# Turning the attention output with VectorE and five transfers through DRAM instead of TensorE transposes

## The chip, the cores and the metric

The kernel runs on one core of a Trainium2 chip. The metric is device time in microseconds of one execution. Five engines work side by side, each on its own queue in order: TensorE (PE, with its weight loads PEld), VectorE (DVE), ScalarE (ACT), GpSimd (POOL) and SyncE (SP). Here SyncE issues nearly all transfers (DMAs), and 16 DMA engines carry them out.

## The reference

```python
B, S, D, Dff = 1, 2048, 576, 4608        # 32 heads of 18, window of 8 keys, dilation 2

xn = layernorm(x)
qkv = xn @ wqkv                          # 576 x 1728
idx = pos[:, None] - 2 * arange(8)       # keys at distance 0, 2, .. 14
attn = softmax(where(idx >= 0, q . k[idx] * 18 ** -0.5, -1e9))
o = sum_w attn * v[idx]
out = x + o @ wo + relu(xn @ w1) @ w2    # w1: 576 x 4608, w2: 4608 x 576
```

All inputs and outputs are float32.

## The kernel before

Rows of x are dealt to two phases (`NPH = 2`, even and odd positions, so that the dilation of 2 becomes a plain window inside a phase). A phase has 1024 rows as 8 tiles `i` of 128 rows, or 4 blocks `tb` of 256 rows. Every float32 factor of a product is split into a high part, rounded to the type float32r, and a low part, the rest; a product is three terms (high by high, low by high, high by low). As D = 576 = 4 x 128 + 64, a left operand of depth 576 is nine 128 x 128 pieces: `d[:, 0:4]` the high parts of the four full pieces, `d[:, 5:9]` their low parts, and `d[:, 4]` the last 64 columns with high parts in partitions 0 to 63 and low parts in 64 to 127. The list `TERMS` has the 14 pairs of pieces that are multiplied.

The time axis is a list of 288 steps (`slots`), 144 a phase: 12 chunks of 3 feed-forward column blocks `f`, over 4 row blocks `tb`. The program is written out by hand in this order. In step n, TensorE does `h_mm(n + 2)` (14 matmuls of 256 columns: a block of x times w1), then what `todo` has for the step, then `o_mm(n)` (12 matmuls of 288 columns: times w2, added up over the three f of a chunk), then what `todo_late` has. `h_mm`'s result is split by ScalarE (`hhi`, line 447) and VectorE (`hlo`, line 448). After f = 2, VectorE adds the chunk's sum to the tile x (line 471). The queues of all engines keep the order of emission.

Weights come through SyncE into `st` tiles (four buffers), three tasks ahead (`AHEAD = 3`), and are split by ScalarE (line 146) and VectorE (line 143) when their step comes: w1 five steps and w2 three steps before the chunk's step, and the five pieces of `wo` eight steps before the output projections. A load is issued when a task ahead of it has been split.

Attention runs on VectorE in four units a phase, as a background list `bg`, which `run_bg` feeds between the other work by an estimate of the time that each engine has been given (`t["pe"]`, `t["dve"]`) and a margin. The result o stands in `QO[ph]`, rows in partitions.

The output projection needs o with its columns in partitions. For each tile, `wo_a` makes a copy of the last 64 columns twice over (`od`, line 411, ScalarE) and calls `transpose_split` (line 264): five transposes of 128 x 128 by TensorE through PSUM (lines 273 and 274), from which ScalarE takes the high parts (lines 276 and 278) and VectorE the rest (lines 277 and 279) into `oT`. `wo_b` then does 28 matmuls of 288 columns, and VectorE adds the two halves to x (line 424). `done` sends a finished tile of x to DRAM.

In a phase that starts at step b, `wo_a(i)` is late in step b + 123 + i, and `wo_b(i)` one step later. In the last chunk of phase 0 (from step 132) the next phase's x is loaded (`load_x`, from step 129), its statistics and norms are taken (`stats`, `norm`, from steps 133 and 134) and it is transposed (`make_xt`, from step 136), on the same PSUM tiles `pm` (two buffers) as `wo_b`. The tile `xn` of `norm` has two buffers, x has 12.

Of the kernel before, what the change touches and what calls it, by code (L numbers as in the profile page):

```python
# [10 lines left out]
F32 = mybir.dt.float32  # L11
F32R = mybir.dt.float32r
AF = mybir.ActivationFunctionType
ALU = mybir.AluOpType
# [3 lines left out]
P = 128  # L18
# [9 lines left out]
EPS = 1e-5  # L28

UNIT0, UNIT_STEP, WO_AT = 7, 27, 8  # L30
HEADW = (-5, -2, -1, 0, 0, 1)

HEAD = (
# [22 lines left out]
def tile_body(ctx: ExitStack, tc: tile.TileContext, x, wqkv, wo, w1, w2, out):  # L56
    nc = tc.nc
    S, D = x.shape
# [5 lines left out]
    KT = 4  # L64
    DR = D - KT * P
    D2 = D // 2
# [4 lines left out]
    ctx.enter_context(tc.manual_schedule())  # L71
    pool = lambda name, bufs, **k: ctx.enter_context(tc.tile_pool(name=name, bufs=bufs, **k))
    consts = pool("consts", 1)
    xp = pool("xp", 12)
    xtp = pool("xtp", NTB)
    qop = pool("qop", 1)
    kp = pool("kp", 1)
# [7 lines left out]
    lgp = pool("lgp", 2)  # L85
    smp = pool("smp", 2)
    tmp = pool("tmp", 2)
    ps_o = pool("ps_o", 2, space=PSUM)
    ps_h = pool("ps_h", 2, space=PSUM)
    ps_m = pool("ps_m", 2, space=PSUM)  # L90

    f32 = lambda ap: ap.bitcast(F32)
# [18 lines left out]
    def mm(o, l, r, start, stop, n):  # L111
        nc.tensor.matmul(o, l, r, start=start, stop=stop)  # L112
        t["pe"] += n / 2400.0 + 0.002

    def dve(n):
        t["dve"] += (n + 130) / 960.0
# [134 lines left out]

    def norm(ph, i, act=False):
        nm, r = MR.pop((ph, i))
        xn = tmp.tile([P, 640], F32, name="xn")
        if act:
            nc.scalar.activation(xn[:, 0:D], X[ph, i], AF.Identity, bias=nm)  # L256
            nc.scalar.activation(xn[:, 0:D], xn[:, 0:D], AF.Copy, scale=r)  # L257
        else:
            nc.vector.tensor_scalar(xn[:, 0:D], X[ph, i], nm, r, op0=ALU.add, op1=ALU.mult)
            dve(600)  # L260
        nc.scalar.activation(xn[:, D:640], xn[:, KT * P : D], AF.Copy)
        XN[ph, i] = xn

    def transpose_split(src, last, hi, mix, lo, free=False):

        if free:
            pa, pb = (ps_o.tile([P, 2, 512], F32, name="po")[:, 0, :] for _ in range(2))
            pa, pb = pa.rearrange("p (k c) -> p k c", k=KT), pb[:, 0:P]
        else:
            pa = ps_m.tile([P, KT, P], F32, name="pm")  # L270
            pb = ps_m.tile([P, P], F32, name="pm")
        for k in range(KT):
            nc.tensor.transpose(pa[:, k, :], src[:, k * P : (k + 1) * P], ident)  # L273
        nc.tensor.transpose(pb, last, ident)  # L274
        t["pe"] += 5 * 0.06
        nc.scalar.activation(hi, pa, AF.Copy)  # L276
        nc.vector.tensor_tensor(lo, pa, f32(hi), op=ALU.subtract)
        nc.scalar.activation(mix, pb, AF.Copy)
        nc.vector.tensor_tensor(mix[DR:P], pb[DR:P], f32(mix[DR:P]), op=ALU.subtract)
        dve(512)  # L280
        dve(128)
# [10 lines left out]
    TERMS = [(k, k) for k in range(KT)] + [(5 + k, k) for k in range(KT)] + [(4, 4)] + [(k, 5 + k) for k in range(5)]  # L292
# [111 lines left out]

    OT = {}

    def wo_a(ph, i):
        assert (ph, i) in ready, (ph, i, len(bg))
        o = QO[ph][:, i, :]
        od = tmp.tile([P, 2, DR], F32, name="od")  # L410
        nc.scalar.activation(od, o[:, None, KT * P : D].to_broadcast([P, 2, DR]), AF.Copy)
        d = tmp.tile([P, 9, P], F32R, name="oT", bufs=1)
        transpose_split(o[:, 0:512], od.rearrange("p a b -> p (a b)"), d[:, 0:4, :], d[:, 4, :], d[:, 5:9, :])
        OT[ph, i] = d

    def wo_b(ph, i):
        d, w = OT.pop((ph, i)), WO[ph]
        po = [ps_m.tile([P, D2], F32, name="pm") for _ in range(2)]
        for j, (a, b) in enumerate(TERMS):
            for h in range(2):  # L420
                mm(po[h], d[:, a, :], w[b][:, h * D2 : (h + 1) * D2], j == 0, j == len(TERMS) - 1, D2)
        for h in range(2):
            acc = X[ph, i][:, h * D2 : (h + 1) * D2]
            nc.vector.tensor_tensor(acc, po[h], acc, op=ALU.add)
            dve(D2)
# [53 lines left out]
    def at(n, f, *a):  # L479
        todo.setdefault(n, []).append((f, a))  # L480
# [3 lines left out]
    def late(n, f, *a):  # L484
        todo_late.setdefault(n, []).append((f, a))

    plan = []
    for ph in range(NPH):
        b = ph * SPP
        for c in range(NCH):  # L490
            for f in range(C):
                s = b + c * SPC + f
                first = ph == c == 0
                plan.append((HEADW[f] if first else s - 5, w1_task, ((ph, c, f), c * C + f)))
                plan.append((HEADW[3 + f] if first else s - 3, w2_task, ((ph, c, f), c * C + f)))
        for u in range(NU):
            s = b + UNIT0 + u * UNIT_STEP
            plan.append((s - 5, wq_tasks, ((ph, u), u)))
            for i in range(NI):
                at(s + i, qkv_tile, ph, u, i)  # L500
            late(s + NI + 1, attention, ph, u)
        s = b + UNIT0 + NU * UNIT_STEP + WO_AT
        plan.append((s - 8, wo_tasks, (ph,)))
        for i in range(NI):
            late(s + i, wo_a, ph, i)
            at(s + i + 1, wo_b, ph, i)
            at(s + i + 1, done, ph, i)
        if ph + 1 < NPH:
            e = b + SPP - SPC
            for i in range(NI):  # L510
                z = e + 3 + 2 * i
                at(z - 6, load_x, ph + 1, i)
                late(z - 2, stats, ph + 1, i)
                late(z - 1, norm, ph + 1, i)
                at(z + 1, make_xt, ph + 1, i)
# [16 lines left out]
    held = []  # L532
    run_splits(-5)
    norm(0, 0)
    norm(0, 1)
    stats(0, 2)
    make_xt(0, 0)
# [48 lines left out]
```

## Time and profile before

| | |
|---|---|
| Time, median of 3 runs | 1194.78 us (1194.58 to 1195.4) |
| Profiled execution | 1194.74 us, span 1193.0 us |
| Mean granted TensorE clock | 0.998 |
| Busy: TensorE / VectorE / ScalarE / GpSimd | 99% / 68% / 26% / 3% |
| DMA, share of 16 engines | 19.7% SyncE's queue, 2.4% ScalarE's |

The span is the time between the first and the last record of the profiled execution; its time by the device's counter is 1.7 us longer. A busy share is an average over the whole span; what a stage waits for is read from that stage's own rows. The chain of waits goes back from the last instruction to what released each one, and so gives the work that set the end.

### The profile page before, as it was taken

How to read it: one execution, taken by the hardware profiler on the slowest of the kernel's cores; microseconds unless marked ns; L12 is line 12 of the kernel's file. 1: busy time of each engine (PE TensorE's matmuls, PEld its weight loads, DVE VectorE, ACT ScalarE, POOL GpSimd, SP SyncE). 2: the span in 40 equal slices, each digit the busy share in tenths (PEclk: the TensorE clock that was granted, in tenths of full speed). 3: DMA queues.
4: the chain of work that ended last, by engine and by line, in shares of the span. 5: the costliest groups of instructions: out<-in, count | busy, mean ns of one | idle time of the engine just before them, and what ended most of it. 6: DMA issues, size and time to landing. Idle time of an engine off the chain costs nothing.

```text
span 1193.0 us, 21739 instructions
## 1 busy us (share of the span) xinstructions
PE 1183.8 (99%) x9016; PEld 1172.8 (98%) x9016; DVE 812.5 (68%) x1269; ACT 310.5 (26%) x790; POOL 40.1 (3%) x63
## 2 busy tenths in 40 slices
PE   8999999999999999999999999999999999999998
PEld 7999999999999999999999999999999999999998
DVE  7516875888687578875573278858767875886732
ACT  5422222131222222322233123122221322222210
POOL 2000000010000000000120000000100000000000
PEclk9999999999999999999999999999999999999999
DMA  5312122130321311402242113031302312212002
GB/s 172 84 32 82 42 76 55 38 107 1 98 58 44 86 33 43 114 11 73 91 130 74 46 54 90 22 85 29 86 21 79 83 38 79 63 42 73 21 1 80
DMA packets 84883, 75.67 MB, mean 63 GB/s; under 512 B 6592, under 2 KB 68288, under 8 KB 84784
## 3 DMA queue, kind: packets, MB, share of 16 engines
q1 hardware_dynamic: 82256, 66.08, 19.7%
q10 hardware_dynamic: 2528, 8.20, 2.4%
q8 instruction: 71, 1.16, 0.4%
q14 instruction: 28, 0.23, 0.1%
HBM read 61.34 MB, written 4.72 MB: 55 GB/s over the span
## 4 chain that ended last, share of the span: by engine, by line
PE 98%; DVE 1%; SPq 0%; ACT 0%; DMA 0%; issue 0%; DVEq 0%; ACTq 0%
PE ph L112 39%; PE po L112 38%; PE pm L112 20%; PE pm L273 1%; PE pm L274 0%; DMA st<-in_w 0%; SPq L235 0%; DVE pr L380 0%; DVE pr L373 0%; SPq L157 0%; SPq L162 0%; SPq L161 0%; PE po L273 0%; ACT xn L257 0%; ACT xn L256 0%
## 5 line engine op out<-in xcount | busy, mean ns | idle before, releaser
L112 PE MATMUL ph<-xT,w1t 128*128 128x256 f32 x4032 | 514.2, 279 | 1.3 <-ACT xT L276 0.6
L112 PEld LDWEIGHTS ph<-xT,w1t 128*128 128x128 f32 x4032 | 491.6, 188 | 2.0 <-ACT xT L276 0.8
L112 PE MATMUL po<-w2t,hhi 128*128 128x288 f32 x2304 | 400.5, 296 | 0.4 <-DVE w2t L143 0.3
L112 PEld LDWEIGHTS po<-w2t,hhi 128*128 128x128 f32 x2304 | 337.0, 188 | 2.0 <-DVE w2t L143 0.5
L447 ACT ACTIVATE hhi<-ph 128x256 fp32r<-128x256 f32 x288 | 110.2, 382 | 531.8 <-PE ph L112 512.5
L112 PE MATMUL po<-w2t,hlo 128*128 128x288 f32 x1152 | 244.7, 293 | 0.0
L448 DVE SCALAR_TENSOR_TENSOR hlo<-ph,hhi 128x256 fp32r<-128x256 f32 x288 | 121.7, 423 | 169.1 <-ACT hhi L447 167.8
L471 DVE TENSOR_TENSOR x<-po,x 128x576 f32<-128x576 f32 x192 | 143.9, 757 | 69.8 <-PE po L112 66.3
L112 PE MATMUL pm<-wq,xT 128*128 128x432 f32 x896 | 185.5, 358 | 0.0
L112 PEld LDWEIGHTS po<-w2t,hlo 128*128 128x128 f32 x1152 | 183.7, 188 | 0.0
L112 PEld LDWEIGHTS pm<-wq,xT 128*128 128x128 f32 x896 | 163.8, 188 | 5.6
L343 DVE TENSOR_TENSOR pr<-qo,k 128x1152 f32<-128x1152 f32 x64 | 85.9, 1349 | 0.0
L373 DVE TENSOR_TENSOR pr<-lg,v 128x1152 f32<-128x1152 f32 x64 | 85.0, 1352 | 0.3
L346 DVE TENSOR_REDUCE lg<-pr 128x64 f32<-128x1152 f32 x64 | 85.0, 1343 | 0.0
L143 DVE TENSOR_TENSOR w2t<-st,w2t 128x576 fp32r<-128x576 f32 x72 | 54.3, 755 | 45.0 <-ACT w2t L146 44.7
L380 DVE TENSOR_TENSOR pr<-pr 128x288 f32<-128x288 f32 (+1 forms) x128 | 70.5, 602 | 0.1
L143 DVE TENSOR_TENSOR w1t<-st,w1t 128x640 fp32r<-128x640 f32 x72 | 59.0, 820 | 15.0 <-ACT w1t L146 14.8
L146 ACT ACTIVATE w2t<-st 128x576 fp32r<-128x576 f32 x72 | 49.1, 684 | 45.0 <-PE po L112 31.0
L146 ACT ACTIVATE w1t<-st 128x640 fp32r<-128x640 f32 x72 | 53.0, 737 | 13.2 <-DMA st<-in_w 13.2
L312 ACT ACTIVATE k<-pm 128x144 f32<-128x144 f32 x64 | 18.7, 292 | 142.8 <-PE pm L112 142.6
L112 PE MATMUL pm<-wq,oT 128*128 128x288 f32 x352 | 51.7, 299 | 0.0
L112 PEld LDWEIGHTS pm<-wq,oT 128*128 128x128 f32 x352 | 47.9, 188 | 1.7
(63 smaller groups left out, 398.0 us busy)
## 6 DMA issues: line engine op xcount, KB each, us to landing
st<-in_w SPq DMA_DIRECT2D x72, 288.0 KB, 3.0
st<-in_w SPq DMA_DIRECT2D x72, 256.0 KB, 3.0
st<-in_wqkv SPq DMA_DIRECT2D x32, 216.0 KB, 3.0
st<-in_w SPq DMA_DIRECT2D x144, 32.0 KB, 2.7
out<-x SPq DMA_DIRECT2D x16, 288.0 KB, 2.1
x<-in_x SPq DMA_DIRECT2D x15, 288.0 KB, 3.9
k<-k ACTq DMA_DIRECT2D x8, 441.0 KB, 3.9
v<-v ACTq DMA_DIRECT2D x8, 441.0 KB, 4.6
```

The costliest lines, as they stand in the source:

```text
L112: nc.tensor.matmul(o, l, r, start=start, stop=stop)
L143: nc.vector.tensor_tensor(lo, src, f32(hi), op=ALU.subtract)
L146: nc.scalar.activation(hi, src, AF.Copy)
L273: nc.tensor.transpose(pa[:, k, :], src[:, k * P : (k + 1) * P], ident)
L312: nc.scalar.activation(k[:, W - 1 + i, :], pq[:, 1, :], AF.Copy)
L343: nc.vector.tensor_tensor(pr[i], q, window(k, i), op=ALU.mult)
L346: nc.vector.tensor_reduce(lg[:, i], pr.pop(i).rearrange(heads, d=Dh), axis=AX.X, op=ALU.add)
L373: nc.vector.tensor_tensor(pr[i].rearrange(heads, d=Dh), e, window(v, i).rearrange(heads, d=Dh), op=ALU.mult)
L380: nc.vector.tensor_tensor(o, z[:, 0:n], z[:, n : 2 * n], op=ALU.add)
L447: nc.scalar.activation(hi, pt, AF.Relu)
L448: nc.vector.scalar_tensor_tensor(lo, pt, 0.0, f32(hi), op0=ALU.max, op1=ALU.subtract)
L471: nc.vector.tensor_tensor(acc, PO[k][:, :, 0:D2], acc, op=ALU.add)
```

## The change

VectorE turns o within 32 x 32 blocks (`nc.vector.transpose`): 576 columns, and the last 64 once more, into one tile `tr` (one buffer). After that, column j of a block is in partition j of the block's group of 32 rows. Four writes, one for each group of 32 partitions, put the blocks into a scratch in DRAM, `turned` (three buffers), at their place in the turned matrix; each write has 32 x 20 runs of 32 floats. A fifth transfer (`wo_f`) reads the scratch back as a tile [128, 5, 128], in runs of 128 floats, into a buffer of the name `xn`. `wo_s` then makes the high parts with one pass of ScalarE and the low parts with two passes of VectorE; the low parts of the four full pieces are written over the fetched tile. `wo_b` is as before.

The four parts of a tile now stand in four steps: `wo_a` late in step z, `wo_f` in z + 1, `wo_s` late in z + 2, `wo_b` in z + 3, where z is b + 123 plus 0, 1, 3, 4, 6, 7, 9, 10 for the eight tiles. So `wo_b` goes from steps b + 124 to b + 131 to b + 126, 127, 129, 130, 132, 133, 135, 136. The name `xn` gets a third buffer, x loses one of 12. The transposes of x (`make_xt`) stay as they are.

```diff
+WO_STEPS = (0, 1, 3, 4, 6, 7, 9, 10)
...
-    xp = pool("xp", 12)
+    xp = pool("xp", 11)
...
+    turned = pool("turned", 3, space=bass.MemoryType.DRAM)
...
-        xn = tmp.tile([P, 640], F32, name="xn")
+        xn = tmp.tile([P, 640], F32, name="xn", bufs=3)
...
     def wo_a(ph, i):
         assert (ph, i) in ready, (ph, i, len(bg))
         o = QO[ph][:, i, :]
-        od = tmp.tile([P, 2, DR], F32, name="od")
-        nc.scalar.activation(od, o[:, None, KT * P : D].to_broadcast([P, 2, DR]), AF.Copy)
-        d = tmp.tile([P, 9, P], F32R, name="oT", bufs=1)
-        transpose_split(o[:, 0:512], od.rearrange("p a b -> p (a b)"), d[:, 0:4, :], d[:, 4, :], d[:, 5:9, :])
-        OT[ph, i] = d
+        tr = tmp.tile([P, 640], F32, name="tr", bufs=1)
+        nc.vector.transpose(tr[:, 0:D], o)
+        nc.vector.transpose(tr[:, D:640], o[:, KT * P : D])
+        dve(D)
+        dve(DR)
+        TD[ph, i] = turned.tile([5 * 4, 32, P], F32, name="turned")
+        for r in range(4):
+            rows = slice(32 * r, 32 * r + 32)
+            nc.sync.dma_start(
+                TD[ph, i][:, :, rows].rearrange("g j i -> j g i"),
+                tr[rows, :].rearrange("j (g i) -> j g i", i=32),
+            )
+
+    def wo_f(ph, i):
+        OT[ph, i] = tmp.tile([P, 5, P], F32R, name="xn", bufs=3)
+        nc.sync.dma_start(f32(OT[ph, i]), TD.pop((ph, i)).rearrange("(k c) j i -> (c j) k i", k=5))
+
+    def wo_s(ph, i):
+        r = OT[ph, i]
+        z = f32(r)
+        d = tmp.tile([P, 5, P], F32R, name="oT", bufs=1)
+        nc.scalar.activation(d, z, AF.Copy)
+        nc.vector.tensor_tensor(r[:, 0:KT], z[:, 0:KT], f32(d[:, 0:KT]), op=ALU.subtract)
+        nc.vector.tensor_tensor(d[DR:P, KT], z[DR:P, KT], f32(d[DR:P, KT]), op=ALU.subtract)
+        dve(512)
+        dve(128)
+        OT[ph, i] = [d[:, k] for k in range(5)] + [r[:, k] for k in range(4)]
...
-                mm(po[h], d[:, a, :], w[b][:, h * D2 : (h + 1) * D2], j == 0, j == len(TERMS) - 1, D2)
+                mm(po[h], d[a], w[b][:, h * D2 : (h + 1) * D2], j == 0, j == len(TERMS) - 1, D2)
...
-            late(s + i, wo_a, ph, i)
-            at(s + i + 1, wo_b, ph, i)
-            at(s + i + 1, done, ph, i)
+            z = s + WO_STEPS[i]
+            late(z, wo_a, ph, i)
+            at(z + 1, wo_f, ph, i)
+            late(z + 2, wo_s, ph, i)
+            at(z + 3, wo_b, ph, i)
+            at(z + 3, done, ph, i)
```

More of the change, by code (lines that the diff above doesn't have):

```diff
@@ L405, in tile_body @@
     OT = {}
+    TD = {}
     def wo_a(ph, i):
```

## The prediction

> **What bounds the kernel now.** I read the page's busy table and chain of waits first, then the chain in order of time around the first group of output projections, then the transfer queue (SyncE's issues, the issue table, the transfer totals of two stretches).
>
> ```profile
> PE 1183.8 (99%) x9016; PEld 1172.8 (98%) x9016; DVE 812.5 (68%) x1269; ACT 310.5 (26%) x790; POOL 40.1 (3%) x63
> ...
> PE 98%; DVE 1%; SPq 0%; ACT 0%; DMA 0%; issue 0%; DVEq 0%; ACTq 0%
> ```
>
> TensorE is the path: 98% of the chain. Whatever is taken off it shortens the run, and whatever makes it wait lengthens it. Next, one step of the stage that is changed (start, length, what):
>
> ```profile
> 502.95 1.59 PE po L112 x12
> 504.54 0.44 PE pm L273 x4
> 504.98 0.11 PE pm L274
> 505.09 1.60 PE ph L112 x14
> 506.69 3.87 PE pm L112 x28
> 510.56 1.58 PE po L112 x12
> ```
>
> A plain step is h_mm 1.61 + o_mm 1.59 = 3.20 us; wo_b adds 3.87. The five transposes of one wo_a lie on the path, 504.54 to 505.09: 0.55 us.
>
> **What is removed.** 16 wo_a at 0.55 us are 8.8 us. Twice (534.99 and 1123.20) the first four take 0.66 instead of 0.44 us, because VectorE came late with L424: 0.4 more. Together 9.2 us off TensorE. That these transposes go is certain, so the change does what it says there; the question is what TensorE waits for instead. The profiled execution took 1194.74 us (span 1193.0 plus 1.7 around it), 0.04 below the median of the runs, so its sum needs no correction. A difference within 0.2% (2.4 us) is about what a measurement of this kernel cannot tell from none.
>
> **What is added for each tile.** The chain is: VectorE transposes; four writes to DRAM on SyncE; SyncE waits until all four have landed, then the fetch; ScalarE's copy; wo_b.
>
> VectorE, transposes: no row shows one. The nearest one-source 576-column pass is L259 at 626 ns, the two-source one is L471 at 757; the 64-column pass is bounded by L279 at 295. I take 0.7 + 0.3 = 1.0 us, with bounds of 0.9 (626 + 295) and of 1.8 (twice L471 plus 295); the upper one would add 0.8 us to each tile's chain. (The Trainium skill, "VectorE: DVE Perf Modes", section on the three transpose paths, gives 311 ns for 128x128 bf16; five of those would be an estimate of 1.6 us, which no run here shows, and would add 0.6 us to each tile's chain.)
>
> VectorE, differences: 512 and 128 columns now from SBUF, like L358 (682) and L279 (295), as much as L277 and L279 today. ScalarE: one 640-column copy, 737 ns by L146, for the 600 + 272 + 304 ns of L276, L278 and L411. VectorE is busy 37.4 us of the 61.2 us from 504.5 to 565.7, so 8 us more fit; they are off the path unless their order holds something back.
>
> The writes decide. The rows:
>
> ```profile
> 480.49 0.38 SPq L157 DMA_DIRECT2D st<-in_w  x1
> 480.91 0.51 SPq L161 DMA_DIRECT2D st<-in_w  x1
> 481.47 0.59 SPq L162 DMA_DIRECT2D st<-in_w  x1
> ```
> ```profile
> st<-in_w SPq DMA_DIRECT2D x72, 256.0 KB, 3.0
> ...
> out<-x SPq DMA_DIRECT2D x16, 288.0 KB, 2.1
> ```
> ```profile
> q1 hardware_dynamic: 1362, 0.65, 49.9%
> ```
> ```profile
> q1 hardware_dynamic: 573, 1.18, 70.6%
> ```
>
> The first fence: back-to-back issues stand 0.57 us apart, so the fourth write starts 1.7 us after the first. The last two are transfer totals (packets, MB, share of 16 engines) of 56.2 to 61 us (w1 loads, 512-byte runs) and of 575 to 580 (x in and out, 2304-byte rows). The first gives 0.499 x 16 x 4.8 / 1362 = 28 ns a packet; the second 56.5 us / 511 long packets = 110 ns. A store of 8 long packets an engine lands after 2.1 us, so about 1.3 us of it is not data.
>
> One tile's writes are 4 x 32 x 20 = 2560 runs of 128 bytes, 160 an engine. No row has a data packet under 512 bytes. Call its time c. The straight line through 28 ns (512 B) and 110 ns (2304 B) gives c = 11; the 512-byte price itself is 28; the dear end is a packet that costs twice the 512-byte one, 56. The nearest row is the 512-byte one, but a quarter of its bytes should not cost all of its time, so I take the middle of it and the line, c = 20. The time from first issue to all landed is W = 1.3 + the larger of (1.7 + 40c) and 160c: 3.4 us at c = 11, 4.5 at 20, 5.8 at 28, 10.3 at 56.
>
> The fetch is 640 runs of 512 bytes, as a w1 load: 3.0 us to landing. With 0.1 us for two handovers and ScalarE's 0.75, a tile is ready for wo_b W + 3.85 after its transposes.
>
> **Where it waits.** Step 123 ends at time 0 of this paragraph (504.5 in the trace). Steps 124 and 125 now hold no wo_b, so TensorE wants wo_b(0) after 2 x 3.20 + 1.61 = 8.0. VectorE can do the transposes by 0.7 (its hlo of that step ended at 504.2). Ready: 0.7 + W + 3.85. The first tile of each phase stalls TensorE by W - 3.4: 1.1 us at W = 4.5.
>
> After that tiles come in pairs. There is one buffer `tr`, so the odd tile's transposes wait for the even tile's writes to land; SyncE sits in wo_f until then too; and wo_s of the odd tile stands ahead of the next pair's transposes on VectorE. A pair's chain closes: transposes 1.0, W, transposes 1.0, W, fetch and copy 3.85, differences 1.0 = 2W + 6.9. TensorE needs 3 x 3.20 + 2 x 3.87 = 17.3 us for a pair. The chain is the shorter while W is under 5.2; at 4.5 it takes 15.9, so 1.4 us is spare. If that cover is gone, each of the three later pairs costs 2W - 10.4.
>
> Behind the waiting instructions: on SyncE, the w2 and x loads of steps 127 to 133. Staging runs three tasks ahead, the load called for at step 127 is split at 129, so one W of delay is covered, at no cost; past that ScalarE's split waits with hhi behind it. On VectorE, hlo and the x adds: hlo is used two steps after its h_mm, and the adds before o_mm with f = 0, where each such step of the stage after 123 holds a wo_b of 3.87 us first. On ScalarE, behind wo_s(0): hhi of step 126, which TensorE, itself held at wo_b(0), does not need yet. One more wait is sure: at step 136 wo_b(7) is now followed by make_xt of the next phase, whose PSUM tile waits for L424 (452 ns): 0.5 us, once. x with 11 buffers: load_x(1,3) waits for the store of X(0,0), 2.1 us on SyncE at a point where the next weight split is four steps away: nothing.
>
> **Sum:** -9.2 + 2 x 1.1 + 0.5 = -6.5, so 1188.2 us. Without any stall (c = 11) it is -8.7, 1186.0; with c = 24, W = 5.1, it is -5.3, 1189.4.
>
> **Rivals.**
>
> *A small packet costs as much as a 512-byte one* (c = 28, W = 5.8). First stall 2.4, then 1.2 for each of three later pairs: 6.0 a phase, 12.0 in all; 1194.7 - 8.7 + 12.0 = 1198, slower. The point from which it decides is W = 5.55 (c = 26.6), where gain and stalls balance; between 5.2 and there the stalls eat the gain. For it: time per packet in the totals falls more slowly than bytes do (28 against 110 ns for 4.5 times the bytes). Against: the line. With c up to 38 (W 7.4: 4.0 + 1.3 + 3 x 4.4 = 18.5 a phase) it reaches 1223.
>
> *Small writes cost double* (c = 56, W = 10.3). The first pair stalls 6.9 and then 4.2 (W + 1.0 against the 7.1 us between two wo_b), each later pair 10.2: 41.7 a phase, 83.4 in all, 1194.7 - 8.7 + 83.4 = 1269. Nothing in the trace shows such packets; the stores of 2304 bytes run at the loads' price, which speaks against it as far as it goes. The Trainium skill, "DMA: Bandwidth & Descriptors", Specifications, speaks for it: a transfer below 512 B is said to be done as a read-modify-write. By that rule this is the time, and no run here shows it yet.
>
> *Order on VectorE.* wo_a and wo_s hold hlo and the attention products while they wait, and TensorE waits for hlo or a free PSUM buffer, beyond the chain above. For it: VectorE was once late for L273 already (the 0.66 us). Against: 24 us of its 61 are idle. It decides once more than those 24 less the 8 added, 16 us a phase, are spent waiting; with W = 4.5 some 2 us a tile, just there. At 3 us a tile, 8 us a phase: 1194.7 - 6.5 + 16 = 1204.
>
> **Chances.** Forecast (W up to 5.3) 0.48. Between there and 5.75, within 0.2% either way: 0.07. Packet as dear as 512 bytes or up to c = 38: 0.22. Doubled or worse: 0.15. Order on VectorE: 0.08. Faster 0.48, same 0.07, slower 0.45. The forecast's own range is 1185.5 to 1190; the 8-in-10 range goes on through c = 38 and the VectorE case, to 1225, and leaves out the doubled packets.
>
> **What would show it.** In the transfer totals of a write stretch: time per 128-byte packet, 20 ns or not. From the first of four issues to SyncE's fetch: W. In TensorE's waits: wo_b waiting for the copy in oT, about 1 us, twice in all, and no other tile. In the chain: no L273 with qo, and VectorE, ScalarE and transfers near 0%. I am wrong if TensorE waits at later tiles too; if then W is under 5.2, it is order; if it is over, it is the packets.

## The result and the profile after

The changed kernel takes 1184.53 us (median; 1183.81 to 1185.6) against 1195.01 us for the kernel before, measured beside it: a ratio of 0.9913, 95% interval 0.9903 to 0.9923. That is 10.5 us faster, where 6.5 were forecast; the time lies 1.0 us under the low end of the range. The profiled execution took 1184.46 us with a span of 1182.7, 10.3 us shorter than before.

Busy times and the chain of waits on the page of the changed kernel:

```profile
PE 1174.6 (99%) x8936; PEld 1164.9 (98%) x8936; DVE 822.3 (70%) x1301; ACT 306.9 (26%) x758; POOL 40.1 (3%) x63
...
PE 95%; DVE 2%; DMA 2%; ACT 0%; SPq 0%; issue 0%; POOL 0%; DVEq 0%; ACTq 0%
```

TensorE has 80 instructions less (16 x 5 transposes) and is still the path. A few per cent of the chain run over VectorE and transfers now; that is where the first tile of each phase comes in just late. The chain in order of time (start, length, what), first tile and second:

```profile
503.97 0.69 DVE tr L417
504.66 0.12 DVE tr L418
504.78 0.35 DVE pr L382
...
506.34 2.04 DMA turned<-tr
...
508.53 3.07 DMA xn<-turned
511.59 0.02 issue
511.62 0.75 ACT oT L438
512.36 0.04 issue
512.41 3.98 PE pm L114 x28
516.38 1.59 PE po L114 x12
517.97 1.60 PE ph L114 x14
519.57 3.72 PE pm L114 x28
```

The chain of the prediction is there in its order: transposes, writes, fetch, copy, wo_b. The first wo_b takes 3.98 us on this chain, which counts it from the end of the copy. For TensorE the wait is longer: its first matmul starts 0.33 us after the last one of h_mm (0.53 in the second phase) where the later tiles' start after 0.11, and the second comes 0.24 us later instead of 0.13. So the first tile loses 0.3 us in the first phase and 0.5 in the second. The second wo_b takes 3.72, and so do the later ones until the phase's last. Before, a wo_b took 3.87. That difference is what the prediction did not see.

SyncE's queue at the same place, and the issue table:

```profile
504.81 2.07 SPq L424 DMA_DIRECT2D turned<-tr  x4
508.53 0.38 SPq L431 DMA_DIRECT2D xn<-turned  x1
509.44 2.12 SPq L424 DMA_DIRECT2D turned<-tr  x4
513.61 0.38 SPq L431 DMA_DIRECT2D xn<-turned  x1
519.42 2.79 SPq L424 DMA_DIRECT2D turned<-tr  x4
```
```profile
turned<-tr SPq DMA_DIRECT2D x64, 80.0 KB, 2.3
xn<-turned SPq DMA_DIRECT2D x16, 320.0 KB, 3.2
```

From the first issue (504.81) to the fetch (508.53), W is 3.7 us; four issues take 2.07 of it. The transfer totals (packets, MB, share of 16 engines) of 504.8 to 508.6 us:

```profile
q1 hardware_dynamic: 2624, 0.33, 49.5%
```

0.495 x 16 x 3.8 us / 2624 = 11.5 ns for a packet of 128 bytes (the count holds 64 packets more than the 2560 runs, 16 for each write): the value on the straight line, 11, and not the 20 that was taken.

The one place where TensorE waits longer is the end of phase 0:

```profile
570.61 3.60 PE pm L114 x27
574.22 0.02 issue
574.24 0.47 DVE x L453
574.71 0.04 issue
574.75 0.66 PE pm L275 x4
```

make_xt's transposes wait for the first of L453's two passes, which frees the first of the two PSUM tiles. The second tile costs nothing: its transpose (L276) starts at 575.25, 0.11 us after the fourth of L275. From the last matmul of wo_b (574.04) to that fifth transpose it takes 1.2 us, where 0.6 would do without the wait. The loss is 0.6 us.

### The profile page after: what moved, and what is told of

It reads as the page before. It is cut to its first block, busy times and chain, and to the rows that moved or that the text cites. A ratio compares the mean times of both kernels' runs of the same rounds, so it can differ in the third digit from the quotient of the medians.

```text
span 1182.7 us, 21731 instructions
## 1 busy us (share of the span) xinstructions
PE 1174.6 (99%) x8936; PEld 1164.9 (98%) x8936; DVE 822.3 (70%) x1301; ACT 306.9 (26%) x758; POOL 40.1 (3%) x63
## 4 chain that ended last, share of the span: by engine, by line
PE 95%; DVE 2%; DMA 2%; ACT 0%; SPq 0%; issue 0%; POOL 0%; DVEq 0%; ACTq 0%
PE ph L114 37%; PE po L114 37%; PE pm L114 20%; DMA st<-in_w 1%; DMA xn<-turned 1%; PE pm L275 0%; DVE pr L382 0%; DMA turned<-tr 0%; DVE x L500 0%; DMA x<-in_x 0%; DVE pr L345 0%; SPq L424 0%; DVE w1t L145 0%; DVE w2t L145 0%; DVE bst L245 0%
## 5 line engine op out<-in xcount | busy, mean ns | idle before, releaser
L500 DVE TENSOR_TENSOR x<-po,x 128x576 f32<-128x576 f32 x192 | 143.4, 756 | 69.9 <-PE po L114 67.0
L351 POOL TENSOR_SCALAR_AFFINE_SELECT lg<-lg 1x512 f32<-1x512 f32 x8 | 9.4, 1171 | 844.1 <-DVE lg L348 844.1
L114 PE MATMUL pm<-wq,oT 128*128 128x288 f32 x224 | 35.2, 296 | 0.3 <-ACT oT L438 0.3
```

The costliest lines, as they stand in the source:

```text
L351: nc.gpsimd.affine_select(out=z, in_=z, pattern=[[1, NI], [1, W], [0, HG]], compare_op=ALU.is_ge, fill=-1e9 / scale, base=1 - W, channel_m ...
L500: nc.vector.tensor_tensor(acc, PO[k][:, :, 0:D2], acc, op=ALU.add)
```

## The experiments

Theory A came from the single matmuls of a wo_b before. Most start 0.13 us after the one ahead, but the second and third come 0.18 and 0.24 us after theirs: 0.15 us are lost at the first write to the second PSUM tile `pm`. VectorE's L279 of the same tile's transposes reads that tile until just then: it ends at 514.27, wo_b starts at 514.14 and its second matmul at 514.33. The timelines of TensorE (start, length of two matmuls from there on) and VectorE:

```profile
514.14 0.58 PE L112 MATMUL pm<-wq,oT 128*128 128x288 f32 x2
514.33 0.52 PE L112 MATMUL pm<-wq,oT 128*128 128x288 f32 x2
```
```profile
513.26 0.69 DVE L277 TENSOR_TENSOR oT<-pm,oT 128x512 fp32r<-128x512 f32 x1 [1.96 <-ACT oT L276]
513.98 0.29 DVE L279 TENSOR_TENSOR oT<-pm,oT 64x128 fp32r<-64x128 f32 x1
```

The second matmul reads only high parts (`TERMS` begins with the pair 0, 0), so it is the PSUM tile it waits for, and not what L279 writes. The view of waits does not list it: the first matmul is recorded until 514.44, so TensorE has no idle time there. Three runs of the kernel before test it.

**e1_two_steps.** Transposes kept, tiles two steps apart:

```diff
-            late(s + i, wo_a, ph, i)
-            at(s + i + 1, wo_b, ph, i)
+            late(s + 2 * i, wo_a, ph, i)
+            at(s + 2 * i + 2, wo_b, ph, i)
...
```

> The kernel before, TensorE transposes kept, but the tiles stand two steps apart and wo_b two steps after wo_a (wo_a late in s + 2i, wo_b in s + 2i + 2), so that a whole step lies between the transposes and the 28 matmuls. Theory A (wo_b of the kernel before holds a wait: its second matmul needs the second PSUM tile pm, which VectorE's L279 still reads, about 0.15 us for each tile): wo_b falls from 3.87 to 3.72 us, 16 x 0.15 = 2.4 us less, 1192.4; the transposes stay at 0.55 us each. Rival B (the matmuls are faster because the operand oT has 5 slots instead of 9, or its low parts lie in another tile): wo_b stays at 3.87, time 1194.8.

Measured: 1192.46 us, ratio 0.9981 (0.9972 to 0.999). The chain around one tile:

```profile
515.10 0.44 PE pm L273 x4
515.53 0.11 PE pm L274
...
520.46 3.72 PE pm L112 x28
```

All 16 wo_b take 3.72 us with the old operand and with the transposes on TensorE. So the operand's place (B) is not it; the distance from the transposes is.

**e2_no_L279.** The instruction that holds the tile is taken away, and nothing else is moved. The kernel leaves out the low parts of the last 64 columns of o:

```diff
...
+        if low64:        # False in wo_a
             nc.vector.tensor_tensor(mix[DR:P], pb[DR:P], f32(mix[DR:P]), op=ALU.subtract)
```

> The kernel before without VectorE's L279 in wo_a (the low parts of the last 64 columns of the attention output are left out, the partitions hold the high parts instead); order and steps unchanged. Theory A (L279 holds the second PSUM tile): wo_b 3.72 us at once, 2.4 us less, 1192.4. Rival B (operand's place): 3.87, 1194.8. Rival C (wo_b waits for VectorE's other pass L277 or for data, not for the PSUM tile): wo_b stays above 3.8.

Measured: 1192.36 us, ratio 0.9981 (0.9972 to 0.999), and 3.72 us for every wo_b one step behind its transposes:

```profile
511.39 0.44 PE pm L273 x4
511.82 0.11 PE pm L274
513.54 3.72 PE pm L112 x28
```

L277 and the copies were left in, so C is out. The holder is L279.

**e3_steps_only.** The change's spacing alone, each wo_a in the step just ahead of its wo_b:

```diff
+            z = s + (0, 1, 3, 4, 6, 7, 9, 10)[i]
+            late(z + 2, wo_a, ph, i)
+            at(z + 3, wo_b, ph, i)
...
```

> The kernel before with only the spacing of the change: wo_b at the change's steps (z + 3, z = s + 0, 1, 3, 4, 6, 7, 9, 10), wo_a late in the step just before it. Theory A: the wait goes with the transposes one step ahead, so wo_b stays at 3.87 us and the time at 1194.8 (at most 0.5 us less, where L424 no longer delays the transposes). Rival D (the spacing itself, with plain steps between, lets VectorE keep up and is worth the extra 2 us): 1192.5 or less.

Measured: 1196.63 us, ratio 1.0017 (1.0008 to 1.0025), 2.1 us slower. Most wo_b stay at 3.87. The third tile's in each phase starts 0.6 us late and takes 4.0, as VectorE's attention work stands ahead of its L277 in the chain, and the last of phase 0 ends in the clash with make_xt. Spacing alone gains nothing (D falls); what was not expected is that it costs something.

**e10_transposes_twice.** The first term by itself: the kernel before with each set of five transposes done twice.

```diff
+        for _ in range(times):        # 2 in wo_a
             for k in range(KT):
                 nc.tensor.transpose(pa[:, k, :], src[:, k * P : (k + 1) * P], ident)
             nc.tensor.transpose(pb, last, ident)
```

> The kernel before with the five transposes of each wo_a done twice over, into the same PSUM tiles. Theory (each set of five lies bare on TensorE at 0.55 us, and the wait at wo_b's second matmul stays what it is, since the chain behind the transposes only starts later): 16 x 0.55 = 8.8 us more, 1203.5, wo_b 3.87. Rival (part of the 0.55 us is cover for VectorE or ScalarE, so that taking the transposes away gives less): 5 us more or less, 1199 or under.

Measured: 1203.35 us against 1194.84 beside it, ratio 1.0072 (1.0059 to 1.0086): 8.5 us more for 16 sets, 0.53 each. The term is right in size.

**e5_writes_twice.** The chain's cover, tested with a longer W:

```diff
-            nc.sync.dma_start(TD[ph, i][:, :, rows]..., tr[rows, :]...)
+            for dst in (twin, TD[ph, i]):
+                nc.sync.dma_start(dst[:, :, rows]..., tr[rows, :]...)
```

> The changed kernel with each of the four writes issued twice, to a second scratch that nothing reads as well: 8 issues, 5120 runs of 128 bytes a tile. The changed kernel has W = 3.7 us from first issue to all landed; eight issues 0.54 us apart make the last start at 3.8, so W = 5.9. Theory (the prediction's chain law, with wo_b at 3.72: a pair's chain 2W + 6.9 against 17.0 us of TensorE): first tile +2.2, three later pairs 1.7 each, 7.3 us a phase, 1184.5 + 14.5 = 1199. Rival (only the first tile of a phase is exposed, all later ones are covered): 1184.5 + 4.4 = 1189. Rival (double price of a small write): packets far above 11.5 ns and W over 8, 1215 or more.

Measured: 1207.48 us against 1194.6, ratio 1.0105 (1.0092 to 1.0119): 23 us over the changed kernel, more than the 14.5 of the chain law. The first W is 6.05 us (504.94 to 510.99), near the 5.9 expected. The later ones are longer. SyncE's queue:

```profile
523.83 0.30 SPq L427 DMA_DIRECT2D twin<-tr  x1
...
528.58 0.54 SPq L427 DMA_DIRECT2D turned<-tr  x1
529.22 0.49 SPq L160 DMA_DIRECT2D st<-in_w  x1
529.75 0.54 SPq L164 DMA_DIRECT2D st<-in_w  x1
530.34 0.59 SPq L165 DMA_DIRECT2D st<-in_w  x1
531.10 0.47 SPq L434 DMA_DIRECT2D xn<-turned  x1
```

Three weight loads stand between the writes and their fetch, so that W is 7.3 us here and 6.8 at the pair's second tile. From a pair's first write to that of the next pair it takes 18.9, 20.9 and 20.2 us in the first phase and 18.9, 20.9 and 19.1 in the second, where TensorE needs 3 x 3.20 + 2 x 3.72 = 17.0. The pair law with each place's own two W (their sum + 6.9) gives 19.1, 20.9, 20.4 and 19.0, 20.4, 19.0: it holds within 0.5 us. Over the 17.0 these six stretches cost 17 us; the longer W of the two first tiles costs 4.6 and the last tile of each phase 1.7 together, which makes the 23 measured. So the expected 14.5 failed on the W of the later pairs and not on the law, and the rival of a single exposed tile falls. In the changed kernel W grows in the same way, from 3.7 to 5.1 us (519.42 to 524.53), and stays covered: its longest pair (W of 5.0 and 4.6) needs 16.4 of the 17.0.

**e6_runs_64B.** Each write cut into two of 64-byte runs:

```diff
+            for q in range(2):
+                half = slice(32 * r + 16 * q, 32 * r + 16 * q + 16)
                 nc.sync.dma_start(
-                    TD[ph, i][:, :, rows]..., tr[rows, :]...
+                    TD[ph, i][:, :, half]..., tr[rows, :]...[:, :, 16 * q : 16 * q + 16]
```

> The changed kernel with each write cut into two of 64-byte runs: 8 issues, 5120 runs of 64 bytes a tile, half the bytes of the kernel that writes everything twice. Theory (time per packet goes on falling along the straight line through 512 and 2304 bytes): 7 to 9 ns a packet, W held by the eight issues at 5.9, time as with doubled writes, 1199. Rival (a packet has a floor near 11.5 ns): 11 to 12 ns, W and time about the same. Rival (below 128 bytes a write is done twice over): 20 ns or more, W over 7.5 and time over 1210.

Measured: 1208.03 us (one run), as with the doubled writes (1207.48); both miss the 1199 that stood on a W of 5.9 at every tile. Transfer totals of 504.8 to 510.9 us, first of the doubled writes (128 bytes), then of this kernel (64 bytes):

```profile
q1 hardware_dynamic: 5248, 0.66, 61.9%
```
```profile
q1 hardware_dynamic: 5248, 0.33, 44.4%
```

11.5 and 8.3 ns a packet. Half the bytes cost less time on the engines and none less at the end: the first W is 5.9 us here and 6.1 there, with eight issues in both. No floor at 11.5 ns, and no double price.

**e4_first_earlier.** The changed kernel with its two remaining waits aimed at:

```diff
-WO_STEPS = (0, 1, 3, 4, 6, 7, 9, 10)
+WO_STEPS = (-1, 1, 3, 4, 6, 7, 9, 10)   # wo_b(0) stays in its step
...
-                at(z + 1, make_xt, ph + 1, i)
+                (at if i else late)(z + 1, make_xt, ph + 1, i)
```

> The changed kernel with its two remaining waits taken away: the first tile's wo_a, wo_f and wo_s one step earlier (wo_b where it was), and make_xt of the next phase's first tile after o_mm instead of before it. Theory: 0.26 us less at each phase's first wo_b and 0.7 us less at make_xt, together 1.2 us: 1183.3, against 1184.5 of the changed kernel. Rival (the waits only move, since the first tile's chain is behind VectorE's attention work): 1184.5 and a wo_b of 3.98 again.

Measured: 1189.52 us, ratio 0.9957 (0.9945 to 0.997): 5 us slower than the changed kernel. wo_s(0) is now late in the same step as wo_a(1) and ahead of it. VectorE's timeline (in brackets the idle time before, and what ended it):

```profile
511.01 0.69 DVE L439 TENSOR_TENSOR xn<-xn,oT 128x512 fp32r<-128x512 f32 x1 [4.81 <-ACT oT L438]
511.73 0.29 DVE L440 TENSOR_TENSOR oT<-xn,oT 64x128 fp32r<-64x128 f32 x1
512.05 0.78 DVE L417 STREAM_TRANSPOSE tr<-qo 128x576 f32<-128x576 f32 x1
```

VectorE idles 4.8 us for the first tile's fetch, and the second tile's transposes start at 512.05 instead of 508.51. TensorE then waits for the copies of the later tiles, 4.6 us in three waits, and 1.4 us in two for their differences (L439).

**e8_xt_late.** Only the second of the two edits, make_xt behind o_mm.

> The changed kernel with one line moved: make_xt of the second phase's first tile stands after o_mm of its step, instead of before it and right behind the last wo_b. Theory (its PSUM tile waits for L453's two passes): 0.7 us less, 1183.8. The earlier run with the first tile moved as well lost 5 us; if this one alone keeps 1183.8, the loss is the first tile's, whose wo_s then stands ahead of the second tile's transposes on VectorE. Rival (the loss came from make_xt's move): 1189.

Measured: 1183.43 us against 1194.6 beside it, ratio 0.9908 (0.9894 to 0.9921): 11.2 us under the kernel before, where the changed one is 10.5 under it. The intervals overlap; in the chain of this run make_xt follows o_mm with no wait, 0.44 us for its first four. The loss of e4 was therefore the first tile's.

**e9_order.** e4 with the two entries of that step swapped:

```diff
-            late(z + 2, wo_s, ph, i)
+            if i:
+                late(z + 2, wo_s, ph, i)
+            if i == 1:
+                late(z, wo_s, ph, 0)        # behind wo_a(1)
...
```

> The kernel of e4_first_earlier (first tile one step earlier, make_xt late) with two entries of one step swapped: wo_a of the second tile stands ahead of wo_s of the first, so that VectorE does the second tile's transposes before it waits for the first tile's fetch. Theory (e4 lost because these transposes stood behind that wait): the loss of 5 us goes, and the first stall of 0.26 us a phase too: 0.5 us under e8_xt_late, 1182.9. Rival (the first tile came too early for the attention work still queued on VectorE): about 1189 as e4, with TensorE waiting at the second and third wo_b.

Measured: 1183.3 us against 1194.84 beside it, ratio 0.9903 (0.9889 to 0.9917). The loss is gone, and VectorE does the second tile's transposes first:

```profile
507.69 0.78 DVE L417 STREAM_TRANSPOSE tr<-qo 128x576 f32<-128x576 f32 x1 [1.12 <-DMA turned<-tr]
...
511.65 0.69 DVE L439 TENSOR_TENSOR xn<-xn,oT 128x512 fp32r<-128x512 f32 x1 [3.05 <-ACT oT L438]
```

All 16 wo_b take 3.72 us, and the output projections no longer wait at all. The further 0.5 us does not show in the time: in this run TensorE waited 1.1 us for L500 in the second phase, outside the stage. It does show inside. In the chains, count each stage from an h_mm ahead of its first transposes to an o_mm behind its last wait (in the kernel before, 498.14 to 587.56 and 1083.21 to 1184.19). The two stages together are 10.1 us shorter in the changed kernel, 10.9 in e8 and 11.5 in e9. By their whole times e8 and e9, the best versions, cannot be told apart.

**e7_x_too.** Six tiles of the second phase's x by the same way, the other two by make_xt as in the changed kernel:

```diff
+                if i in X_TURNED:               # 0, 1, 2, 3, 4, 6
+                    late(z - 1, x_a, ph + 1, i) # transposes and writes
+                    at(z + 1, x_f, ph + 1, i)   # fetch
+                    late(z + 2, x_s, ph + 1, i) # high and low parts
```

> The changed kernel with six of the eight x tiles of the second phase (0, 1, 2, 3, 4, 6) turned in the same way: transposes on VectorE late in step z - 1, four writes, the fetch in z + 1, the split late in z + 2. Theory: each tile takes 0.55 us of transposes off TensorE, and nothing waits for PSUM at the first one: 6 x 0.55 + 0.7 = 4.0 us less, 1180.5. Rival (the waits of VectorE and SyncE hold back norms, hlo or the weights in a stage where VectorE is fuller): 1184.5 or more, with TensorE waiting for hlo, xT or w1t between 580 and 640 us.

Measured: 1192.86 us, ratio 0.9981 (0.9972 to 0.999): 8 us slower than the changed kernel instead of 4 faster. The tiles stand two steps of 3.2 us apart here, with no wo_b between them, and SyncE also carries x in, x out and weights. Waits of TensorE from 555 to 640 us:

```profile
PE po L115 <- DVE x L521: 5.4, 2, 3.7
PE ph L115 <- DVE xT L281: 0.6, 1, 0.6
PE ph L115 <- DVE hlo L498: 0.6, 1, 0.6
```

The fetch lands after 4.6 us instead of 3.2 (median between 570 and 632 us), and the x adds stand on VectorE behind the wait for it. These waits are 6.6 us, and about 8 counted from matmul to matmul. Behind the longest of them TensorE also runs slower: the rows below (length of the stretch, busy time, granted clock, DMA share, GB/s) show a granted clock of 0.50, and from 617.0 to 622.5 the matmuls of o_mm stand 0.24 us apart instead of 0.13. That is nearly 3 us more.

```profile
607.00:613.00 6.00, 6.00 (x52) 1.00 0.66 225
616.00:622.00 6.00, 5.04 (x22) 0.50 0.31 54
```

Less the 3.9 us that the six sets of transposes and the wait at make_xt were worth, this makes the 7 us that the stage loses against the changed kernel. Most of the rest is the first wo_b of the second phase, which waits 1.6 us by the view of waits, where 0.3 are listed in the changed kernel.

## Why the prediction was wrong

The direction held, and so did the mechanism of the detour; the size did not, because one wait that the change removes was taken for work. Step by step:

- *Removed, 9.2 us.* Right: no transposes of `qo` are left, and doing them twice costs 8.5.
- *wo_b adds 3.87 us.* **This step failed.** The 3.87 was taken for the matmuls' own time, before and after. It held 0.15 us of waiting for L279 on the second PSUM tile, and that went away with the transposes: 3.72, over 16 tiles 2.3 us (e1, e2). The sum had no term for it. The row was there to be checked: o_mm's 12 matmuls of the same 288 columns take 1.59 us, which makes 3.71 for 28.
- *Small writes, c = 20 ns, W = 4.5, first stall 1.1 us a phase.* Mis-sized: c is 11.5 and W 3.7 (the formula for W gives 3.5 with this c), and the stall is 0.3 us in the first phase and 0.5 in the second. That is 1.4 us. The end of the range that came from the straight line was the right one, and the middle with the 512-byte price was not. The rival of the doubled price did not come: a packet of 128 or 64 bytes took less time than one of 512 bytes, though a byte in it took more (0.09 ns at 128 bytes, 0.055 at 512). That rival leaned on the read-modify-write that the Trainium skill states in "DMA: Bandwidth & Descriptors", Specifications, for transfers below 512 B. The measured times decide against a doubling of time here; whether there is a read-modify-write, no run here shows.
- *VectorE's transposes, 1.0 us.* Measured 0.78 + 0.20. The estimate of 1.6 us from the figure of the Trainium skill, "VectorE: DVE Perf Modes", The three transpose paths, does not hold for these forms.
- *Pairs covered while W is under 5.2.* Right: no later tile waits, with W between 3.6 and 5.1, and e5 shows the law beyond it. With wo_b at 3.72 the bound is 5.05 for the mean of a pair's two W, which is at most 4.8. The weight loads in SyncE's queue, held to cost nothing, lengthen W; that costs nothing while the cover lasts, and time once it is gone (e5).
- *make_xt, 0.5 us.* 0.6, one wait, as forecast.
- *Order on VectorE.* Not in the changed kernel, but near: one step's shift of one tile brings it about and costs 5 us (e4, e9).

In the profile's terms: -9.2 - 2.3 + 0.8 + 0.6 = -10.1. That is what the two stages lost (4.9 and 5.2 us by the marks named under e9); the other 0.2 us of the span's 10.3 lie ahead of the first stage. With c on the line alone the sum would have been 1186.0; it took the wait inside wo_b to get under 1185.5.

## What to carry to other kernels

Before pricing what is removed, compare what stays with the same work elsewhere per instruction: a group that is 4% dearer than its twin can hold a wait, as here, and this wait for a PSUM buffer inside a running series of matmuls stood in no list of waits. A detour over DRAM was free here once its whole chain, with what stands between its issues in the queue, fitted the time that the bound engine needs per tile; compute that chain per pair of tiles, with each buffer that closes it. Where an in-order engine both starts a later tile and waits for an earlier one in the same step, put the start ahead of the wait.

## What the runs showed of the hardware

The time per packet fell nearly on a straight line down to short writes: 110 ns for 2304 bytes, 28 for 512 (loads), 11.5 for 128 and 8.3 for 64 (writes). Four writes of 128-byte runs were issued 0.4 to 0.6 us apart: the fourth began 1.5 us after the first and its landing took 2.0 more, while their packets filled half of the 16 engines' 3.8 us. VectorE turned 576 float32 columns in blocks in 0.78 us, close to a two-input pass of 576 columns (0.757). Behind one wait of 3.7 us (e7) TensorE's granted clock was 0.50 for 5.5 us; of e5's waits of about 3 us, one in the second phase was followed by 3.4 us at 0.52 and those ahead of 515.0 and 535.3 by none.
